# The head of a two-layer attention and mixer kernel, put into another order: tokens first, then each weight ahead of its own matmuls, the other loads tied to steps

## The chip, the cores and the metric

The kernel runs on one core of a Trainium2 chip. The metric is device microseconds for one execution of the whole program, the median of several executions. Five engines work side by side, each on its own list of instructions in its own order: TensorE (PE in the profile, its weight loads PEld), VectorE (DVE), ScalarE (ACT), GpSimd (POOL) and SyncE (SP), which issues all DMA transfers of this kernel. An instruction that waits holds everything behind it on its engine.

## What is computed

Four sublayers follow one another on 2048 tokens of width 640: attention A, mixer B, A again with the same weights, B again. Each is added to its input, and each takes a normalised input.

```python
x = x + A(layernorm(x)); x = x + B(layernorm(x))
x = x + A(layernorm(x)); x = x + B(layernorm(x))

# A: 32 heads of 20, four segments of 512 tokens, one after another
for s in range(4):
    p = softmax(q_s k_s^T * scale + mask)            # within the segment
    a_mem = phi(q_s) M / (phi(q_s) z + 1e-6)         # memory of the segments before
    o_s = g * a_mem + (1 - g) * (p v_s)
    M, z = M + phi(k_s)^T v_s, z + sum(phi(k_s))
y = o @ wo
# B: z1, z2 = halves of gelu(x @ w_in);  y = (z1 * (w_sp @ layernorm(z2) + b_sp)) @ w_out
```

## The kernel before, in words

**Precision.** A matmul of float32 precision is made of three float16 matmuls. Every operand is split into a high half and a low half: the high half is the float16 of the scaled value, the low half what is left. A weight's scale is a power of two taken from its largest absolute value. For one weight this takes (lines 48 to 73): a reduction of each 128-row piece, a reduction over the pieces (`wam`), `pow2_scales` with a transpose and a small matmul on TensorE (`wtp`, `wbc`, lines 52 and 58) and some eight tiny VectorE operations that end in `iv` (line 65), and then per piece one ScalarE operation for the high half (line 72) and one VectorE operation for the low half (line 73).

**Head.** `prologue` (line 117) loads wv, wq and wk, in that order, each as five tiles of 320 KB (line 135), and scales and splits them in the order v, q, k (lines 136 to 145). It then derives some scalars from the scales of q and k (lines 150 to 165). In `Attention.run`, for the first layer (`self.stacked < 0`, line 1030), `prep` loads 128 tokens (line 607), takes statistics (line 202, then a power on POOL, line 205), normalises (line 615), splits (line 217 on ScalarE, 218 on POOL) and turns the halves by a transposing DMA (line 219, tile `xt`). `start` fills the constant rows of the five `qk` buffers (lines 585 and 586). Then `early` computes four value tiles (`value`, line 621) and units 0 and 1 (`unit`, line 678).

**Units and values.** A unit m of segment s is 128 feature columns of q and of k for 512 tokens: 15 matmuls for q, then 15 for k (line 689). Both accumulate in the PSUM pool `pd`, tag `dn`, two banks. `out` (line 694) evicts them: high half on ScalarE, low half on VectorE, and for k the feature map phi too (lines 705, 711, 713, 722, 723), which writes into the bank in place and so holds it until line 723 is done. The halves go to a buffer in DRAM (`stack`, lines 798 and 799). A value tile is 128 tokens by 640 columns in two halves of 15 matmuls (line 632), also in `dn`.

**The step loop.** The 64 pairs of heads are worked off in steps t, three steps for each pair, from t = -10 (`-LEAD`) on. `fetch` (line 803) brings the pair's q and k rows into one of five `qk` buffers. `scores` (line 829) makes, for pair n, score blocks in `es` (one pair of banks, `pe`) which ScalarE turns into exponentials `P` (line 864), and, two pairs ahead, blocks in `mp` (one pair of banks, `px`) whose row maxima VectorE takes (`mx`, line 871). `maxes` (line 885) sends the maxima into the `qk` buffer by two small DMAs (line 894). `cast` splits `P` into `PH` (ScalarE, line 881) and `PL` (POOL, line 882); `pvs` multiplies with the values (line 908).

Beside the steps run four streams, each with a due time in steps: `fills` (token preps and the reads of `o`), `background` (the scales and splits of the remaining weights), `dense` (the units, values and output projections of later segments, in an order written out by hand, with a pace in ns of matmul per step) and `reads` (the memory). `until` (line 1043) takes what is due.

`background` begins at step 6. In the first layer `other_scales` (line 168) loads 32 tiles of wo, w_in and w_out (`wmst`, line 179, two buffers) and reduces each on VectorE (`wap`, lines 181 and 185), at 1.2 steps from tile to tile in program order; at step 53 come the scales, from step 55 on the splits of `wo` and of the second half of `w_in`.

**What sets the order.** Only TensorE follows the program's order (`manual_schedule(engines=ENGINES)`, line 1085). For the other engines and for the DMA queue of SyncE a planner orders the instructions when the program is built: it takes, among those that it believes ready, the one that was traced first, and `high_priority` makes instructions count as traced earlier. So in the kernel before, the 32 `wmst` loads, which wait for nothing but their two buffers, were put far ahead of step 6: the trace has the first reduction at 23.9 us and the last at 112.7 us.

## Time and profile before

| what | value |
|---|---|
| timed executions | 2472.66, 2474.31, 2476.86 us; median 2474.31 |
| span of the profiled execution, from the first to the last instruction | 2466.8 us |
| median less the span (what lies around it) | 7.5 us |
| instructions in the profile | 50722 |
| first value matmul | 36.17 us |
| first unit of step -10 | 88.30 us |
| first score matmul of step 0 | 134.39 us |

The profile is of one execution, with its own times in us from the start of the span; the page has no other time of that execution than the span. A row of the timeline gives start, duration, engine, line and operation, the tile written and read, how many instructions were merged, and in brackets how long the engine stood idle before and what released it. Line L207 means line 207 of the kernel. SPq rows are the issues of DMAs, not the transfers.

### The profile page before, as it was taken

What the parts mean: (1) busy time and instruction counts of PE and PEld (TensorE: products, weight loads), DVE (VectorE), ACT (ScalarE), POOL (GpSimd) and SP (SyncE); (2) the same over time, 40 slices, a digit from 0 to 9 for tenths busy, and PEclk for the clock granted to TensorE, in tenths of its full rate; (3) what the DMA queues carried; (4) which work ended last, traced back from release to release, by engine and by line L of the source; (5) the groups of instructions that cost most, each with busy time, mean ns of one, the idle gap of its engine ahead of it and who ended that gap; (6) DMA issues with size and microseconds to landing.
All of it is one profiled execution on the core that took longest, in us unless ns stands there. A gap on an engine that the chain in (4) does not pass through costs nothing.

```text
span 2466.8 us, 50722 instructions
## 1 busy us (share of the span) xinstructions
PE 2224.2 (90%) x20682; PEld 1317.4 (53%) x20682; DVE 1431.5 (58%) x2766; ACT 1137.3 (46%) x1388; POOL 937.1 (38%) x728
## 2 busy tenths in 40 slices
PE   3688888999899989999997888889997997999998
PEld 2355455666545545555554545565664554555554
DVE  8667877677754545544326777777764453453441
ACT  3278767777632222212124977777772222121110
POOL 3168777888610100000012988788872110000000
PEclk9899899999999999999999999999998998999999
DMA  6724644334553487767444352443446345766762
GB/s 198 207 56 101 172 107 113 100 108 123 140 162 94 114 221 193 189 155 173 101 137 124 74 123 69 112 113 86 126 128 145 94 114 151 167 166 155 173 128 58
DMA packets 502505, 325.00 MB, mean 132 GB/s; under 512 B 408512, under 2 KB 443456, under 8 KB 497152
## 3 DMA queue, kind: packets, MB, share of 16 engines
q1 hardware_dynamic: 502272, 321.76, 50.8%
q8 instruction: 162, 2.65, 0.5%
q14 instruction: 71, 0.58, 0.1%
HBM read 148.25 MB, written 85.34 MB: 95 GB/s over the span
## 4 chain that ended last, share of the span: by engine, by line
PE 56%; DVE 10%; ACT 10%; DMA 9%; issue 5%; SPq 3%; POOL 3%; ACTq 0%; DVEq 0%; POOLq 0%
PE gp L380 16%; PE zp L295 13%; PE cyp L409 6%; ACT PH L881 3%; ACT P L864 3%; PE vps L632 3%; PE pv L908 3%; DVE mx L871 3%; DMA wr<-in_B_w_sp_dram 2%; PE kps L689 2%; PE mp L855 2%; PE qps L689 2%; PE yps L665 2%; PE es L855 2%; POOL PL L882 2%
## 5 line engine op out<-in xcount | busy, mean ns | idle before, releaser
L882 POOL TENSOR_TENSOR PL<-P,PH 128x1280 f16<-128x1280 f32 x248 | 649.6, 2619 | 177.0 <-ACT PH L881 156.4
L380 PE MATMUL gp<-zh,wt 128*128 128x432 f16 x2048 | 466.6, 348 | 23.8 <-DMA wt<-wn 23.8
L871 DVE TENSOR_REDUCE mx<-mp 128x2 f32<-128x1024 f32 (+3 forms) x512 | 409.4, 816 | 130.2 <-PE mp L827 127.4
L380 PEld LDWEIGHTS <-wt 128*128 128x128 f16 x3072 | 301.8, 98 | 286.4 <-DMA wt<-wn 25.5
L864 ACT ACTIVATE P<-es,sc 128x1024 f32<-128x1024 f32 (+1 forms) x384 | 371.3, 967 | 161.6 <-PE es L827 160.0
L881 ACT CAST PH<-P 128x1280 f16<-128x1280 f32 x256 | 320.5, 1253 | 19.2 <-PE pv L908 12.8
L295 PEld LDWEIGHTS <-th 128*128 128x128 f16 x1920 | 188.6, 98 | 178.6 <-issue 10.4
L380 PE MATMUL gp<-zl,wt 128*128 128x432 f16 x1024 | 272.8, 348 | 0.0
L395 POOL MEMSET un<- 128x64 f16 x32 | 4.8, 151 | 672.5 <-DMA ut<-un 610.2
L205 POOL TENSOR_TENSOR lnrs<-lnve,mhalf 128x1 f32<-128x1 f32 x96 | 58.5, 617 | 467.7 <-DVE lnve L204 442.9
L855 PEld LDWEIGHTS <-qk 60*128 60x128 f16 (+1 forms) x2048 | 91.4, 93 | 261.3 <-issue 155.6
L383 ACT ACTIVATE u<-gp,bsp,un 128x864 f32<-128x864 f32 x32 | 34.2, 1070 | 363.3 <-PE gp L380 363.3
L357 DVE TENSOR_REDUCE am<-wr 128x1 f32<-128x2048 f32 x32 | 73.2, 2286 | 218.6 <-DMA wr<-in_B_w_sp_dram 218.6
L855 PE MATMUL mp<-qk 60*128 60x512 f16 (+3 forms) x1024 | 138.3, 307 | 55.9 <-DVE mx L871 55.0
L632 PE MATMUL vps<-wvh,xt 128*128 128x320 f16 x640 | 157.5, 310 | 27.2 <-DMA xt<-xnhl 14.5
L409 PE MATMUL cyp<-wuh,ut 128*128 128x320 f16 (+1 forms) x896 | 166.8, 303 | 11.9 <-DMA ut<-un 11.9
L855 PE MATMUL es<-qk 64*128 64x512 f16 (+3 forms) x1024 | 134.3, 298 | 47.3 <-ACT P L864 34.7
L409 PEld LDWEIGHTS <-ut 128*128 128x128 f16 (+1 forms) x1344 | 132.8, 99 | 69.9 <-DMA ut<-un 13.5
L827 PEld LDWEIGHTS <-big 64*128 64x128 f16 x3072 | 141.0, 95 | 50.5 <-issue 3.2
L908 PE MATMUL pv<-vs,PL 128*128 128x41 f16 x2560 | 163.0, 181 | 4.9 <-DVE PL L882 2.6
L908 PE MATMUL pv<-vs,PH 128*128 128x41 f16 x2560 | 166.3, 182 | 1.2 <-DVE ab L924 1.2
L295 PE MATMUL zp<-wi1h,th 128*128 128x432 f16 x640 | 150.2, 349 | 8.8 <-DMA th<-xnhl 8.8
(182 smaller groups left out, 4063.7 us busy)
## 6 DMA issues: line engine op xcount, KB each, us to landing
wr<-in_B_w_sp_dram SPq DMA_DIRECT2D x32, 1024.0 KB
qk<-st SPq DMA_DIRECT2D x256, 120.0 KB
x<-x SPq DMA_DIRECT2D x56, 320.0 KB
z<-z SPq DMA_DIRECT2D x32, 432.0 KB
cz<-z SPq DMA_DIRECT2D x32, 432.0 KB
xt<-in_A_x_dram SPq DMA_DIRECT2D x32, 320.0 KB
st<-qhl SPq DMA_DIRECT2D x40, 256.0 KB
st<-khl SPq DMA_DIRECT2D x40, 256.0 KB
```

The source lines that it names most:

```text
L295: nc.tensor.matmul(zp[:, n, :FHH], a[:, k, :], b[:, k, c:c + FHH], start=(k == 0 and j == 0), stop=(k == KD - 1 and j == 2))
L380: nc.tensor.matmul(gp[:, n, :FHH], wt[:, k // 8, a, k % 8, :], b[:, k, n * FHH:(n + 1) * FHH], start=(k == 0 and j == 0), stop=(k == NT - ...
L409: nc.tensor.matmul(yp[:, n, :320], a[:kn[k], k, :], b[:kn[k], k, n * 320:(n + 1) * 320], start=(k == 0 and j == 0), stop=(k == KO - 1 and ...
L632: nc.tensor.matmul(ps, a[:, k, c], b[:, k, n * 320:(n + 1) * 320], start=(i == 0), stop=(i == 14))
L689: nc.tensor.matmul(ps, a[:, k, c], b[:, k, :], start=(i == 0), stop=(i == 14))
L827: nc.tensor.matmul(out, g.big[r, 64 - 64 * s:192 - 64 * s], mk, start=False, stop=s == 1, skip_group_check=True)
L855: nc.tensor.matmul(out[:, h, o:o + w], a[r, ac], b[r, bc], start=o == 0, stop=False, skip_group_check=True)
L864: nc.scalar.activation(P[:, :, 512 * c:512 * c + ew], es[:, :, :ew], AF.Exp, scale=g.esc)
L871: nc.vector.tensor_reduce(self.mx[m][:, :, i], mp[:, :, o:o + w], AX.X, ALU.max)
L881: nc.scalar.copy(PH, P[:, h])
L882: (nc.gpsimd if h == 0 or n < self.N - self.TAIL else nc.vector).tensor_tensor(PL, P[:, h], PH, ALU.subtract)
L908: nc.tensor.matmul(pv[:, i, h, :], x[:, c:c + 128], v[:, j, h0 + h, :], start=(j == 0 and x is PH), stop=(j == i and x is PL), skip_group_ ...
```

## The change

The head is a new method of `Attention`, `head`, which takes the place of `prologue`'s loads and splits and of the first layer's `prep`, `start` and `early`.

- *Order of loads on SyncE*: four token tiles into one buffer `xs` (a buffer of `P`), the five tiles of wq, the first two turns, the five tiles of wk, the other two turns, then wv. wk is issued after the second turn and wv after the fourth (`issue_after` adds an order without a wait on data, on the engine that issues).
- *Tokens* are normalised and split into `xhl`, one buffer for all four tiles (a second buffer of `P`).
- *q* is scaled and split after the second token tile in program order. Then TensorE has q's matmuls of units 0 and 1, both m, in the bank pair of `es`; then k's scale, split and matmuls in the bank pair of `mp`; then v's scale and split, `start`, and the four value tiles in `dn`.
- *The split of k and v*: pieces 1 and 3 of five are done as a multiplication in place and a copy on ScalarE and a subtraction on POOL, instead of one ScalarE and one VectorE operation.
- *The rest*: the scalars (`attn_scalars`) come after k's split; the load of `bsp` and the clearing of `wap` move to step 6; the interval of `other_scales` becomes 1.45 steps; what the streams `fills` and `background` issue on SyncE is put behind the last fetch or row of maxima traced so far, in both layers; the pools `topi` and `topo` are opened after the head instead of before.

```diff
-def prologue(g, ctx, wv, wq, wk, wo, w_in, w_out):
+def attn_weights(g, ctx, wv, wq, wk, wo, w_in, w_out):
...
+    def head(self):
+
+        g, nc, tc = self.g, self.nc, self.tc
+        abs_max = lambda out, a: nc.vector.tensor_reduce(out, a, AX.X, ALU.max, apply_absolute_value=True)
+        with ExitStack() as ctx:
+            p = ctx.enter_context(tc.tile_pool(name="wpro", bufs=1, side="right", reuse_waits="tile"))
+            ctx.enter_context(tc.high_priority(offset=HP))
+            xs = self.p3.tile([128, 4, D], F32, tag="P", name="xs")
+            hl = self.p3.tile([128, 4, 2, D], F16, tag="P", name="xhl")
+            for t in range(4):
+                nc.sync.dma_start(xs[:, t], self.x[t])
+            st = {nm: p.tile([128, KD, D], F32, name="wst" + nm) for nm in "qkv"}
+
+            def load(nm):
+                for k in range(KD):
+                    self.sp = nc.sync.dma_start(st[nm][:, k, :], g.raw[nm][k * 128:(k + 1) * 128, :]).ins
+
+            def scale(nm):
+                i = WNAMES.index(nm)
+                am = g.wam[:, i:i + 1]
+                a = p.tile([128, KD], F32, tag="wamk", name="wamk")
+                for k in range(KD):
+                    abs_max(a[:, k:k + 1], st[nm][:, k])
+                nc.vector.tensor_reduce(am, a, AX.X, ALU.max)
+                pow2_scales(g, self.pl1, self.pm, "ms", g.wam, i, 1)
+
+            def split(nm):
+                h, l = g.w[nm]
+                for k in range(KD):
+                    if nm == "q" or k % 2 == 0:
+                        split_scaled(g, h[:, k], l[:, k], st[nm][:, k], WNAMES.index(nm))
+                    else:
+                        w = st[nm][:, k]
+                        nc.scalar.mul(w, w, g.iv[:, WNAMES.index(nm):][:, :1])
+                        nc.scalar.copy(h[:, k], w)
+                        nc.gpsimd.tensor_tensor(l[:, k], w, h[:, k], ALU.subtract)
+
+            last = None
+            for t in range(4):
+                mv, rs = layernorm_stats(g, xs[:, t], D, 2, XS)
+                nc.vector.tensor_scalar(xs[:, t], xs[:, t], mv[:, 0:1], rs, ALU.subtract, ALU.mult)
+                nc.scalar.copy(hl[:, t, 0], xs[:, t])
+                nc.gpsimd.tensor_tensor(hl[:, t, 1], xs[:, t], hl[:, t, 0], ALU.subtract)
+                o = self.xt[0][:, :, :, t * 128:(t + 1) * 128]
+                if t % 2 == 0:
+                    with tc.issue_after(last) if last is not None else ExitStack():
+                        load("qk"[t // 2])
+                last = nc.sync.dma_start(o.rearrange("p i k c -> p (i k) c"), hl[:, t].rearrange("p i c -> p (i c)"), transpose=True).ins
+                if t == 1:
+                    scale("q")
+                    split("q")
+            with tc.issue_after(last):
+                load("v")
+            qp = self.pe.tile([128, 2, 512], F32, tag="es", name="qp")
+            kp = self.px.tile([128, 2, 512], F32, tag="mp", name="kp")
+            for nm, ps in (("q", qp), ("k", kp)):
+                if nm == "k":
+                    scale("k")
+                    split("k")
+                    attn_scalars(g)
+                for m in range(2):
+                    for _ in self.unit(0, m, {nm: ps[:, m]}):
+                        pass
+            scale("v")
+            split("v")
+            self.start()
+            for t in range(4):
+                for _ in self.value(t):
+                    pass
...
-        for nm in ("q", "k"):
+        for nm in ("q", "k") if own is None else own:
             wh, wl = g.w[nm]
-            ps = self.pd.tile([128, L], F32, tag="dn", name=f"{nm}ps")
+            ps = self.pd.tile([128, L], F32, tag="dn", name=f"{nm}ps") if own is None else own[nm]
...
             if not g.wo.made:
+                nc.sync.dma_start(g.bsp, self.b_sp.rearrange("(t p) -> p t", p=128))
+                nc.vector.memset(g.wap, 0.0)
                 for i, _ in enumerate(other_scales(g, self.bg, self.pl1, self.pm, "ms")):
-                    yield 6 + 1.2 * i if _ else 53
+                    yield 6 + 1.45 * i if _ else 53
...
         if self.stacked < 0:
-            for t in range(0, 4, 2):
-                for f in zip(self.prep(t), self.prep(t + 1)):
-                    f[0]()
-                    f[1]()
-                if t == 0:
-                    self.start()
-            for i in range(4, 8):
-                self.early(i)
+            self.head()
         else:
             self.start()
+        g = self.g
+        g.top = [self.top.enter_context(g.tc.tile_pool(name=n, bufs=1, side="right", reuse_waits="tile")) for n in ("topi", "topo")][::-1]
...
-                e[0] = next(e[2], None)
+                with self.tc.issue_after(self.sp) if e[1] < 2 and self.sp is not None else ExitStack():
+                    e[0] = next(e[2], None)
```

In `fetch` and `maxes`, `self.sp` is set to the DMA that was just issued.

58 lines of the change are left out of this document (21 added, 37 removed).

## The prediction

> **What bounds the kernel now.** I read the page first, then the busy times by stage, then the timeline of the first 140 us engine by engine, then the waits, and last the same stages of the second attention layer, which the program enters around 1290 us without the loads that this change moves.
>
> The page's first line says that TensorE is busy 90% of the span. So time can be had only where it stands still, and the busy times by stage say where (columns: stretch, its length, then busy us of PE, PEld, DVE, ACT, POOL with counts, granted clock, DMA share, GB/s).
>
> ```profile
> PE 2224.2 (90%) x20682; PEld 1317.4 (53%) x20682; DVE 1431.5 (58%) x2766; ACT 1137.3 (46%) x1388; POOL 937.1 (38%) x728
> ...
> 0.00:36.20 36.20, 4.46 (x16) 3.18 (x17) 33.08 (x88) 9.76 (x14) 8.42 (x28) 1.00 0.69 217
> 36.20:88.30 52.10, 36.24 (x181) 19.38 (x181) 35.77 (x88) 17.91 (x30) 18.17 (x19) 0.90 0.78 198
> 88.30:134.40 46.10, 34.14 (x206) 16.56 (x206) 25.24 (x42) 8.66 (x16) 0.55 (x1) 0.85 0.59 163
> 134.40:240.00 105.60, 92.24 (x1409) 56.39 (x1405) 78.47 (x149) 92.09 (x116) 86.87 (x48) 0.98 0.34 82
> 1292.30:1335.80 43.50, 31.68 (x202) 15.60 (x200) 26.46 (x51) 11.19 (x20) 7.79 (x8) 0.88 0.62 157
> ```
>
> Until 36.2 us TensorE does almost nothing while VectorE is full (33.1 of 36.2). From 36.2 to 88.3 it does the four value tiles and units 0 and 1; from 88.3 to 134.4 it leads in (steps -10 to -1); at 134.4 the first scores of step 0 start. Everything after is a chain on that start. The boundaries, in the timeline (start, us, engine, line, operation, and the wait in brackets):
>
> ```profile
> 36.17 0.45 PE L632 MATMUL vps<-wvh,xt 128*128 128x320 f16 x1 [9.23 <-DMA xt<-xnhl]
> 88.30 0.59 PE L689 MATMUL qps<-xt,wqh 128*128 128x512 f16 x2
> 88.95 0.59 PE L689 MATMUL qps<-xt,wqh 128*128 128x512 f16 x2
> 134.39 0.38 PE L855 MATMUL es<-qk 64*128 64x512 f16 x2
> ```
>
> The first value matmul waits for the first turned tokens, not for a weight. 88.30 to 88.95 is the price of three unit matmuls at full clock, 0.65 us; a unit's fifteen for q or k take 3.2 us.
>
> **The change part by part.** *Head.* The same work in another order: tokens, then q, then k, then v. TensorE's order is the program's, so the rise has three links in a row: q's matmuls, k's scale, split and matmuls, v's scale, split and matmuls. The durations:
>
> ```profile
> 9.82 0.16 DVE L139 TENSOR_REDUCE wam<-wamk 128x1 f32<-128x5 f32 x1
> 14.98 0.14 DVE L65 TENSOR_SCALAR iv<-iv 128x1 f32<-128x1 f32 x1
> 5.30 0.82 DVE L138 TENSOR_REDUCE wamk<-wstv 128x1 f32<-128x640 f32 x1
> 9.00:12.00 3.00, 0.58 (x2) 0.29 (x3) 3.00 (x9) 0.00 (x0) 0.00 (x0) 1.00 1.03 404
> 28.98 0.88 DVE L73 SCALAR_TENSOR_TENSOR wql<-wstq,iv,wqh 128x640 f16<-128x640 f32 x1
> 36.86 3.70 ACT L72 ACTIVATE wkh<-wstk,iv 128x640 f16<-128x640 f32 x5
> 37.03 1.40 POOL L218 TENSOR_TENSOR xnhl<-xt,xnhl 128x640 f16<-128x640 f32 x1 [4.40 <-ACT xnhl L217]
> 57.77 1.33 SPq L219 DMA_TRANSPOSE xt<-xnhl  x1
> 61.18 0.31 PE L632 MATMUL vps<-wvh,xt 128*128 128x320 f16 x1 [1.42 <-DMA xt<-xnhl]
> 61.32 0.30 PE L632 MATMUL vps<-wvl,xt 128*128 128x320 f16 x1
> 61.73 0.30 PE L632 MATMUL vps<-wvl,xt 128*128 128x320 f16 x1
> 109.67 1.01 PE L689 MATMUL kps<-xt,wkh 128*128 128x512 f16 x2 [8.34 <-DVE phl L723]
> 110.91 1.06 PE L689 MATMUL kps<-xt,wkh 128*128 128x512 f16 x2
> ```
>
> q: the first transfer can be reduced at 5.3 us, and at 404 GB/s a 320 KB tile lands each 0.82 us; q's five stand behind four of tokens, so the ninth is in at 11.9 and reduced at 12.7. The scale chain took 5.3 us for v (9.82 to 15.1): 18.0. The split is paced by VectorE, five of 0.88 us after ScalarE's first 0.74: 23.1. The tokens: POOL's 1.40 us subtraction and a 3.4 us turn (57.77 to 61.18) end each tile, and tiles 2 and 3 are written behind q's scale and split, so I put the last turned tile at 25 us; q's matmuls need all four. Thirty matmuls take 6.5 us, and after a long idle time three cost 1.24 us instead of 0.65 for some 4 us (109.67 to 110.91), 1.8 more: **33**.
>
> k: its loads wait on SyncE behind the second turn, at some 13 us, and land by 20 (five of 0.82, and the turns between); v's, behind the fourth, by 30. Both are early. But its two small matmuls of the scale follow q's on TensorE: the chain begins at 33; fewer other VectorE operations are left, 4 us: 37. The split puts seven ScalarE operations of 0.74 us in a row (two of five pieces take a multiplication and a copy), then 0.88 on VectorE: the first k unit ends at 43.3, the second, partly at the low clock, at **48**.
>
> v: chain again, now beside the k units' eviction on VectorE, 5.3: 53.3. The first half value is paced by the split, 6.3: 59.6. Seven halves of fifteen (three cost 0.41 us, 61.32 to 61.73) take 14.4, the low clock about 2: **76**. Against 88.3 that is 12 us earlier. Bounds: 66, if the chains overlap better (3 us each, as no filler stands between their operations), and 84, if each is as long as k's was:
>
> ```profile
> 24.66 0.14 DVE L139 TENSOR_REDUCE wam<-wamk 128x1 f32<-128x5 f32 x1
> 36.43 0.14 DVE L65 TENSOR_SCALAR iv<-iv 128x1 f32<-128x1 f32 x1
> ```
>
> That was 11.9 us, with splits and reductions between every two of its operations. I take 76, since v's own chain (5.3) is the nearest row.
>
> The early units in the scores' banks cost nothing: the scores ask for them only in the lead-in, and they spare the value tiles a wait for a bank. The new copies on ScalarE are in the sum. The fill of the `qk` buffers moves behind v's split:
>
> ```profile
> 38.41 4.59 POOL L586 TENSOR_SCALAR qk<-wkh,keep 128x512 f16<-128x512 f16 x5
> 42.42 3.17 ACT L585 ACTIVATE qk<-wkh,qrow 128x512 f16<-128x512 f16 x5 [1.53 <-DVE qrow L158]
> ```
>
> It lies beside 14 us of value matmuls; without them the first fetch would come 4.6 us later. `bsp`'s load and the clearing of `wap` only change place. The first prep of the next tokens goes behind the first fetch; v4 is 5 steps later, so a 3.3 us load is covered; without that cover TensorE would wait those 3.3 us.
>
> *Lead-in, 46.1 us now.* Here the weights' loads are in the way today:
>
> ```profile
> 102.06 0.82 DVE L181 TENSOR_REDUCE wap<-wmst 128x1 f32<-128x640 f32 x1 [5.54 <-DMA wmst<-in_B_w_out_dram]
> PE kps L689 <- DVE phl L723: 17.7, 4, 8.3
> L181 DVE TENSOR_REDUCE wap<-wmst x31: 547/603/821, 23.9 to 111.4; 128x1 f32<-128x432 f32 x20, 128x1 f32<-128x640 f32 x11
> ```
>
> VectorE stands 5.5 us for a load, and behind it waits the k eviction that frees a bank. Yet the same stage in layer 2 has no such loads and takes 43 us (1292.3 to 1335.1, the table's last row): another wait ends last there. So only some **4 us** go.
>
> *First segment, 105.6 us now.* The 32 reductions come here, at 1.45 steps apart from step 6. There are 31 in the row above and one more of 96 partitions: twenty at its median of 0.6 us, twelve at its 0.8, 21.6 us in all, 1.4 us per pair of heads. VectorE goes from 78.5 to 100.1 of 105.6 us. It is the engine that frees the one bank pair of `mp`, and TensorE stands in order behind that:
>
> ```profile
> PE mp L855 <- DVE mx L871: 6.3, 13, 1.0
> 135.25 1.12 ACT L864 ACTIVATE P<-es,sc 128x1024 f32<-128x1024 f32 x1
> 239.10 1.11 ACT L864 ACTIVATE P<-es,sc 128x1024 f32<-128x1024 f32 x1 [2.78 <-PE es L827]
> ```
>
> Fifteen pairs take 103.9 us, 6.9 each. At 95% use, a reduction often stands just ahead of a maximum. Each reduction also comes some 3 us after its own load (1.45 steps of 2.3), and a load of this size needs 3.4 us from issue to reader:
>
> ```profile
> 270.19 0.59 SPq L607 DMA_DIRECT2D xt<-in_A_x_dram  x1
> 273.60 0.89 DVE L202 BATCH_NORM_STATS2 lnst<-xt 128x6 f32<-128x320 f32 x2 [0.76 <-DMA xt<-in_A_x_dram]
> ```
>
> so some of them will make VectorE stand. Bounds: 2 us lost (all in its 27 us of idle time) and 34 (21.6 added whole, and 0.4 of standing each). I take **9**, two fifths of the work.
>
> Ahead of the reductions in SyncE's queue now stand the fetch and the row of maxima; a blocked fetch holds the load, and the load holds a reduction. Behind step 53 the loads of `wo` and `wi1` come at their steps instead of two being early, and layer 2's prep loads may no longer run ahead: I take 0 for both, bounds 3 either way, for a token load is read 3.4 us after its issue and has 11 steps.
>
> The sum: 12 + 4 - 9 = 7 us less. The profiled span is 2466.8, the median 2474.3; the 7.5 us around the span stay. Span 2460, time **2467**.
>
> *A rule weighed.* VectorE and POOL do collide in this trace:
>
> ```profile
> 328.76 2.62 POOL L882 TENSOR_TENSOR PL<-P,PH 128x1280 f16<-128x1280 f32 x1
> 328.92 2.92 DVE L73 SCALAR_TENSOR_TENSOR wi1l<-wst,iv,wi1h 128x432 f16<-128x432 f32 x1
> 398.56 2.62 POOL L882 TENSOR_TENSOR PL<-P,PH 128x1280 f16<-128x1280 f32 x1 [0.81 <-POOL lnrs L205]
> 399.89 0.89 DVE L202 BATCH_NORM_STATS2 lnst<-xt 128x6 f32<-128x320 f32 x2 [1.57 <-DMA xt<-in_A_x_dram]
> ```
>
> An operation with two SBUF operands that starts inside a PL subtraction takes 2.92 us, not 0.6; two statistics with one operand, inside another PL, take their usual 0.89. No row shows a reduction from SBUF under PL, and POOL is in PL four fifths of the first segment. The Trainium skill, "SBUF — State Buffer", section "Who interferes with whom", states that on trn2 a `tensor_reduce` never contends with GpSimd. By that rule the sum stays as it is, and only the loads' half of rival 3 is left.
>
> **The rivals.** (1) *Reductions hidden.* VectorE's 27 us of idle time takes them: loss 2, so 12 + 4 - 2 = 14 less, **2460**; for it, ScalarE (92.1 of 105.6) and TensorE are closer to the bound; against it, TensorE already waits for the maxima. (2) *No difference.* The loss is 16, as most of the moved work lands on the path: **2474**. (3) *Slower, by stalls on VectorE* in the first segment: each of 32 reductions holds VectorE about 1 us more, for its load (3.4 us against 3) or for POOL's port (half of 2.6 us). Then the loss is 21.6 + 32 less some 20 that fall into idle time: 34, so 18 more, **2492**. It decides from a stall of about 0.5 us each. Against it: the statistics row. (4) *The head isn't shorter*: chains of 11.9 us, start at 84: 4 + 4 - 9, **2475**.
>
> **How the numbers follow.** Forecast 0.40 (its own band 2460 to 2472), rival 1 0.20, rival 2 0.14, rival 3 0.16, rival 4 0.10. This kernel's measurement tells about 0.2%, 5 us, from nothing. Of the forecast's 0.40, 0.34 is beyond that and 0.06 within; with rival 1 faster is 0.54. Within: those 0.06, rival 2, and half of rival 4, 0.25. Slower: rival 3 and the other half of rival 4, 0.21. The range goes from 2448 (start at 66, loss 9, lead-in 4, and some) to 2488, which leaves out the far half of rival 3 and the best of rival 1.
>
> **What would show it.** In the changed profile: the first q matmul at about 25 us, the first k at 38, the first value at 54; step -10's first unit (the fifth group of q matmuls, `dn` bank) at 76; first `es` at 118; 32 `wap` reductions spread from step 6 to 51; pairs of the first segment 7.5 us apart instead of 6.9. A first `es` later than 128 would make the head wrong; `wap` reductions of 2 us the port; `wap` waiting for `wmst` by more than 15 us the loads.

## The result and the profile after

The changed kernel takes **2510.2 us** (median of 4 runs, 2502.63 to 2510.85) beside 2473.48 us of the kernel before (4 runs): ratio 1.0148, 95% interval 1.0127 to 1.0170. It is slower by 36.7 us. The forecast was 2467, the range ended at 2488, and the slowest rival stood at 2492. The profiled execution of after took 2509.89 us with a span of 2508.1, so 1.8 us lie around it; before's span was 2466.8, and the spans differ by 41.3. In every execution on record 1.7 to 2.1 us lie around the span: the 7.5 us that I put there for before are mostly that its profiled execution was some 5 us shorter than its median.

The busy times of after by stage (stretch, its length, busy us of PE, PEld, DVE, ACT, POOL with counts, granted clock, DMA share, GB/s), cut where after's own stages end:

```profile
0.00:26.20 26.20, 2.51 (x9) 1.99 (x9) 21.70 (x64) 8.25 (x12) 13.54 (x33) 1.00 0.83 229
26.20:94.20 68.00, 40.73 (x186) 20.44 (x187) 33.63 (x74) 23.02 (x37) 17.38 (x15) 0.75 0.37 101
94.20:131.20 37.00, 33.17 (x207) 16.34 (x206) 16.17 (x26) 7.37 (x14) 0.00 (x0) 0.91 0.24 69
131.20:254.00 122.80, 92.14 (x1373) 56.03 (x1367) 90.93 (x176) 91.97 (x115) 85.45 (x49) 0.96 0.47 121
```

TensorE starts 10 us earlier than before (26.2 against 36.2) and then needs 68.0 us for the matmuls that took 52.1, at a granted clock of 0.75 instead of 0.90: the head is full of holes. Its boundaries in the timeline of TensorE:

```profile
70.46 0.43 PE L689 MATMUL vps<-wvh,xt 128*128 128x320 f16 x1 [3.89 <-ACT wvh L72]
...
94.21 0.59 PE L746 MATMUL qps<-xt,wqh 128*128 128x512 f16 x2
...
131.18 0.38 PE L912 MATMUL es<-qk 64*128 64x512 f16 x2
```

First value matmul 70.5, step -10 at 94.2 (before: 88.3), first scores at 131.2 (before: 134.4). So the start of step 0 moved by 3.2 us, not by 16.

For the rest I follow one row per pair of heads: the start of the pair's last exponential, the only one of 512 columns. A segment has 16 pairs, so pair 15 is the last of the first segment; between pair 41 and the end nothing large happens. Pairs 0, 15 and 41 of layer 1, before and then after, in the timeline of ScalarE:

```profile
139.79 0.68 ACT L864 ACTIVATE P<-es,sc 128x512 f32<-128x512 f32 x1
...
244.04 0.69 ACT L864 ACTIVATE P<-es,sc 128x512 f32<-128x512 f32 x1 [0.47 <-PE es L827]
...
491.51 0.69 ACT L864 ACTIVATE P<-es,sc 128x512 f32<-128x512 f32 x1 [0.70 <-PE es L827]
```

```profile
136.58 0.68 ACT L921 ACTIVATE P<-es,sc 128x512 f32<-128x512 f32 x1
...
262.08 0.69 ACT L921 ACTIVATE P<-es,sc 128x512 f32<-128x512 f32 x1
...
527.12 0.69 ACT L921 ACTIVATE P<-es,sc 128x512 f32<-128x512 f32 x1 [1.29 <-PE es L884]
```

Pairs 0 to 15 take 125.5 us instead of 104.25 (+21.2), pairs 15 to 41 take 265.0 instead of 247.5 (+17.6). After that the two run nearly even: the last pair of layer 2 is 39.6 us late. Three places, then: head and lead-in -3.2, first segment +21.2, the next segments +17.6.

Read in the same rows of each run's own timeline, all runs of this study, as us later (+) or earlier than before at pairs 0, 15, 41 and the last (128th):

| run | what is changed | ratio to before, 95% | 0 | 15 | 41 | last |
|---|---|---|---|---|---|---|
| after | | 1.0148 [1.0127, 1.0170] | -3.2 | +18.0 | +35.6 | +39.6 |
| e2_lag | reductions traced two loads later | 1.0170 [1.0147, 1.0193] | -2.1 | +20.3 | +35.3 | +43.7 |
| e3_no_reduce | no reductions | 1.0039 [1.0024, 1.0055] | -1.9 | -3.8 | +9.0 | +12.6 |
| e12_lag4 | reductions four loads later and behind mx | 1.0088 [1.0073, 1.0103] | -5.0 | -3.7 | +15.4 | +20.4 |
| e9_act_queue | loads on ScalarE's queue | 1.0096 [1.0076, 1.0115] | +10.1 | +7.5 | +21.0 | +26.4 |
| e7_no_hold | nothing held | 1.0033 [1.0020, 1.0046] | +13.9 | +13.7 | +12.4 | +16.5 |
| e6_fills_free | background held alone | 1.0086 [1.0067, 1.0104] | -5.0 | +13.4 | +17.9 | +23.8 |
| e1_bg_free | fills held alone | one execution, 2483.55 us | +10.9 | +8.0 | +15.2 | +15.4 |
| e4_banks | a tile for each head unit | 1.0088 [1.0071, 1.0104] | -12.3 | +5.6 | +23.6 | +26.9 |
| e16_fill | fill behind v's split | 1.0115 [1.0096, 1.0134] | -9.4 | +9.7 | +26.1 | +26.2 |
| e8_before_hold | before, with the hold | 1.0117 [1.0100, 1.0134] | -13.5 | +4.7 | +22.3 | +26.2 |
| b1_before_no_reduce | before, no reductions | 0.9977 [0.9962, 0.9991] | -3.8 | -3.1 | -4.1 | -2.3 |
| e5_lead | e4, loads in the lead-in, nothing else held | 1.0024 [1.0013, 1.0035] | +6.8 | +8.8 | +7.2 | +10.2 |
| e13_mix | e4, e12, less held | 1.0002 [0.9991, 1.0013] | -7.5 | -5.9 | +3.9 | +15.4 |
| e17_all | e4, e16, e12, loads held in segment 1 alone | 1.0053 [1.0036, 1.0070] | -12.4 | +0.2 | +0.9 | +6.9 |
| e18_before_lag | before's head with e17's loads | 0.9986 [0.9974, 0.9999] | -17.6 | -7.3 | -3.3 | +5.5 |

Each row is read from one profiled execution; the farthest from the medians of the timed ones are before's and e17's, some 5 us under, and e13's, 6 above. Runs whose head is the same (after, e2, e3, e12) differ by up to 3.1 us at the first pair, so I read nothing into less than that.

### The profile page after: what moved, and what is told of

Read it like the earlier page. It is cut to its first block, busy times and chain, and to the rows that moved or that the text cites. A ratio compares the mean times of both kernels' runs of the same rounds, so it can differ in the third digit from the quotient of the medians.

```text
span 2508.1 us, 50684 instructions
## 1 busy us (share of the span) xinstructions
PE 2240.5 (89%) x20682; PEld 1327.2 (53%) x20682; DVE 1437.9 (57%) x2762; ACT 1143.2 (46%) x1392; POOL 947.0 (38%) x732
## 5 line engine op out<-in xcount | busy, mean ns | idle before, releaser
L366 PE MATMUL gp<-zh,wt 128*128 128x432 f16 x2048 | 466.6, 348 | 23.8 <-DMA wt<-wn 23.8
L395 PEld LDWEIGHTS <-ut 128*128 128x128 f16 (+1 forms) x1344 | 133.2, 99 | 74.7 <-DMA ut<-un 17.6
L353 ACT ACTIVATE wn<-wr,ivw 128x1024 f16<-128x1024 f32 x64 | 72.0, 1146 | 185.2 <-DVE ivw L348 107.4
```

What stands on the lines that cost most here:

```text
L366: nc.tensor.matmul(gp[:, n, :FHH], wt[:, k // 8, a, k % 8, :], b[:, k, n * FHH:(n + 1) * FHH], start=(k == 0 and j == 0), stop=(k == NT - ...
L395: nc.tensor.matmul(yp[:, n, :320], a[:kn[k], k, :], b[:kn[k], k, n * 320:(n + 1) * 320], start=(k == 0 and j == 0), stop=(k == KO - 1 and ...
```

## The experiments

### The first segment: a loop through two queues

My theory at first: each reduction `wap` of the moved stream stands on VectorE for its own load, and `mx` queues behind it. The waits of after between 131 and 255 us point that way (engine and line, what was waited for: us, times, longest), and the tile's own view gives the reductions' durations:

```profile
PE mp L912 <- DVE mx L928: 25.7, 23, 3.0
...
DVE wap L167 <- DMA wmst<-in_B_w_in_dram: 17.0, 10, 2.2
```

```profile
L167 DVE TENSOR_REDUCE wap<-wmst x31: 553/603/821, 155.5 to 273.8; 128x1 f32<-128x432 f32 x20, 128x1 f32<-128x640 f32 x11
```

VectorE waits 17.0 us in ten stands of up to 2.2 for the pieces of w_in alone (21.3 for all pieces up to pair 15), TensorE stands 25.7 us for `mx` (10.2 in the same stretch of before), and the reductions themselves are as short as before (603 ns).

**e2_lag**: a third buffer, and each reduction traced two loads after its own.

```diff
-                if last is not None:
-                    nc.vector.tensor_reduce(*last, AX.X, ALU.max, apply_absolute_value=True)
-                last = g.wap[:n, i, j:j + 1], t
+                lag.append((g.wap[:n, i, j:j + 1], t))
+                if len(lag) > 2:
+                    nc.vector.tensor_reduce(*lag.pop(0), AX.X, ALU.max, apply_absolute_value=True)
...
```

> After, with each of the 32 reductions wap traced two loads later than its own load (a third staging buffer), so that VectorE's queue reaches a reduction when its data have long landed; the same 32 reductions of 0.60 us stay where they hold up the steps, and the loads stay held to SyncE's steps. Theory A (the pairs 0 to 15 are 21 us longer, 125.5 against 104.3, because VectorE stands some 2.2 us at most reductions for a load issued in the same step, and mx of the next pair queues behind it): the waits of wap on wmst fall from 19.8 us to under 3, the pairs 0 to 15 take 106 to 112 us, the time falls by 14 to 20 to 2490 to 2496. Rival B (the work of the reductions itself, 32 x 0.60 us on a VectorE that sets the pace): the pairs stay at 122 to 126 us, the time at 2507 to 2511.

Nothing changed: 2513.8 us, pairs 0 to 15 take 126.6, and the stands for loads, which were to fall under 3 us, are 19.3 (131 to 256 us). A pair of loads and the reduction of the first of them, in e2's timeline:

```profile
170.30 0.86 SPq L165 DMA_DIRECT2D wmst<-in_B_w_in_dram  x2
...
172.80 0.60 DVE L168 TENSOR_REDUCE wap<-wmst 128x1 f32<-128x432 f32 x1 [1.69 <-DMA wmst<-in_B_w_in_dram]
```

Counted from the first load, the two at 170.30 are the seventh and the eighth, and the reduction at 172.80 is the seventh: the lag is in the program, and on the chip it is gone, since SyncE's queue runs that much behind VectorE's. So e2 did not test its theory; it asked what holds SyncE. One pair of after, in the timeline of all engines:

```profile
168.25 0.51 SPq L951 DMA_DIRECT2D qk<-mr  x1
...
168.86 0.82 SPq L165 DMA_DIRECT2D wmst<-in_B_w_in_dram  x2
...
171.37 0.60 DVE L167 TENSOR_REDUCE wap<-wmst 128x1 f32<-128x432 f32 x1 [2.15 <-DMA wmst<-in_B_w_in_dram]
171.89 1.22 DVE L928 TENSOR_REDUCE mx<-mp 128x2 f32<-128x1024 f32 x1
...
175.64 0.27 DVE L949 SCALAR_TENSOR_TENSOR mr<-mtp,mr 8x128 f16<-8x128 f32 x1
...
175.94 0.52 SPq L951 DMA_DIRECT2D qk<-mr  x1
...
176.50 0.86 SPq L165 DMA_DIRECT2D wmst<-in_B_w_in_dram  x2
...
184.25 0.83 SPq L165 DMA_DIRECT2D wmst<-in_B_w_in_dram  x2
```

This is a **closed loop**. The load stands on SyncE behind the write `qk<-mr` to which the change ties it (168.25, then 168.86). It is read 2.5 us later (171.37). Behind that reduction VectorE does the maxima and, last, the low half of `mr` (175.64). That releases the next write (175.94), and only then the next load goes out (176.50). Once round is 7.64 us, then 7.75 (184.25). Over all 15 intervals of the segment, those with a unit's evictions among them, after needs 8.37 us and before 6.95.

**e3_no_reduce** keeps the 32 loads and leaves the reductions out (the scales of wo, w_in and w_out then come from a constant, so that part of the computation is missing). **e12_lag4** keeps both but puts the reduction four loads behind its load and, by an order on VectorE's own queue, behind the newest `mx`.

```diff
-                if last is not None:
-                    nc.vector.tensor_reduce(*last, AX.X, ALU.max, apply_absolute_value=True)
...
-                nc.vector.memset(g.wap, 0.0)
+                nc.vector.memset(g.wap, 1.0)
```

```diff
+                lag.append((g.wap[:n, i, j:j + 1], t))
+                if len(lag) > 4:
+                    with g.tc.issue_after(g.mxi):
+                        nc.vector.tensor_reduce(*lag.pop(0), AX.X, ALU.max, apply_absolute_value=True)
...
```

> After, with the 32 reductions wap left out and their loads kept in place (the scales of wo, w_in and w_out then come from a constant, so that part of the computation is missing). Theory A (standing for own loads plus the work, both on VectorE): pairs 0 to 15 come down from 125.5 to 103 to 106 us, the time to 2488 to 2491; with e2 it tells the work (the difference of the two) from the standing. Rival C (the 32 loads' transfers, 0.8 us each of SyncE's queue and 221 KB each, hold up the folds and score operands that go by the same queue): pairs stay at 120 or more, time over 2503. The further 17 us of pairs 16 to 41 stay in both.

> After, with each reduction wap traced four loads behind its own load (five staging buffers) and put in VectorE's queue behind the newest reduction mx, so that it can't be drawn forward to its own load as it was in e2; loads, bytes, their hold to SyncE's steps and the 32 reductions of 0.60 us stay. Theory G (per pair a loop: SyncE's write qk<-mr, then the load, its landing 2.5 us later, the reduction wap that VectorE stands for, mx, mr, the next write): the waits of wap on wmst fall from 22.1 us to under 3, pairs 0 to 15 come from 125.5 to 104 to 110 us, the time falls by 14 to 20, to 2489 to 2496. Rival B (the reductions' own 21.6 us on VectorE): pairs stay above 118, time above 2502. What pairs 16 to 41 lose stays in both.

e3: pairs 0 to 15 take 102.35 us, the time is 2481.8; both are a little under what was expected, and pairs 15 to 41 lose 12.8 us where 17 were to stay. So the loads themselves (rival C) cost nothing in the first segment. e12, the timeline at pairs 0 and 15, and its waits between 131 and 255 us:

```profile
134.75 0.68 ACT L923 ACTIVATE P<-es,sc 128x512 f32<-128x512 f32 x1
...
240.39 0.66 ACT L923 ACTIVATE P<-es,sc 128x512 f32<-128x512 f32 x1
```

```profile
PE mp L914 <- DVE mx L930: 9.8, 17, 1.9
...
DVE wap L173 <- DMA wmst<-in_B_w_out_dram: 3.1, 1, 3.1
```

105.6 us with all loads in place and 26 of the 32 reductions inside these pairs (28 in after): 1.4 more than before, 3.3 more than e3. The wait for loads is down to one of 3.1, behind pair 15. It is shown, then, that nearly all of the first segment's 21.2 us comes from where the reductions stood, just behind their own loads and ahead of `mx`, and not from their work. Rival B is out. The stands that went, 21.3 us, are as long as what was won, 19.9; but e12 changes the lag and the place behind `mx` together, and no run tells the two apart. That the stands close into a loop is read off the rows of after; no run opens the loop at SyncE's end.

**e9_act_queue** was to open the loop another way, with the loads on ScalarE's queue (`nc.scalar.dma_start`).

> After, with the 32 loads wmst issued from ScalarE's queue instead of SyncE's, everything else kept (the same hold to the steps, the same 32 reductions, the same bytes). Theory G (a loop once per pair: on SyncE the load stands behind the writes qk<-mr of the step that it is held to, those wait for mr, which comes from mx, and mx stands on VectorE behind the reduction that waits for the load; the loop of 7.6 us sets the pace of pairs 0 to 15): with the load on another queue the loop is open, the waits of wap on wmst fall from 19.8 to under 6 us, pairs 0 to 15 take 106 to 112 us instead of 125.5, and the time comes to 2491 to 2499, with 32 issues of 0.4 us on ScalarE (13 us) as the price that it may show in part. Rival H (the landing of 2.2 to 2.5 us behind any issue, whatever queue): waits and pairs stay, 2505 to 2513.

It missed its purpose. The tile's view:

```profile
L167 DVE TENSOR_REDUCE wap<-wmst x31: 580/603/820, 11.4 to 81.6; 128x1 f32<-128x432 f32 x20, 128x1 f32<-128x640 f32 x11
```

The order behind a SyncE instruction doesn't bind another queue, so all loads ran in the head, and the first pair is 10.1 us late; the first segment, free of them, takes 101.7 us. The time, 2496.9, fell where it was expected, for another reason.

### The hold alone, and what the later segments lose

**e8_before_hold** is before with nothing of the new head, only the hold and the pace of 1.45.

```diff
...
-                e[0] = next(e[2], None)
+                with self.tc.issue_after(self.sp) if e[1] < 2 and self.sp is not None else ExitStack():
+                    e[0] = next(e[2], None)
```

> Before, its head untouched, with the fills and the background stream held behind SyncE's latest step as in after, and the loads wmst at after's pace: the one part of the change that the theory blames, alone. Theory G (the hold makes the loss, whatever the head): pairs 0 to 15 take 118 to 126 us instead of 104.3, pairs 16 to 41 lose 10 to 18, and the time is 2495 to 2508 with a gain of 4 to 8 us before the first pair, whose head then lacks the loads and reductions. Rival (the hold costs only with the new head's queues): 2466 to 2480.

2496.7 us, as theory G has it. In TensorE's timeline its step -10 and its first scores:

```profile
75.15 0.59 PE L690 MATMUL qps<-xt,wqh 128*128 128x512 f16 x2
...
120.92 0.38 PE L856 MATMUL es<-qk 64*128 64x512 f16 x2
```

The first segment loses 18.1 us (21.2 in after) and pairs 15 to 41 lose 17.6, as in after. So the hold makes these losses on the old head too. But the gain ahead of the first pair was put too low: its first scores come at 120.9, **13.5 us ahead of before's and 10.3 ahead of after's**. The old head, freed of the loads and reductions, beats the new one. All of it lies ahead of step -10, which starts at 75.15 instead of 88.30; its lead-in takes 45.8 us, before's 46.1.

**e7_no_hold**, **e6_fills_free** and **e1_bg_free** are after with the hold taken from both streams, from the fills, and from the background (`e[1] < 0`, `e[1] == 1` and `e[1] == 0` in the line above).

> After, with neither the fills nor the background stream held behind SyncE's steps: the new head with the loads placed freely, as before has them. Theory A (hold of the background = +21 in pairs 0 to 15; what is lost in pairs 16 to 41, +17, and in layer 2, +2 to 3, also comes from holding the two streams): the time comes to 2466 to 2476, pairs 0 to 15 take 103 to 108 us. Rival E (the later 17 us come from elsewhere, for instance the changed order of layer 1's evictions or the odd halves of the clock): 2485 to 2492 with the first segment back at 104 to 108. Rival F (free loads crowd into the head): the first es is later than 131.2 by some 10 us and that is lost again.

> After, with only the background stream held to SyncE's steps and the fills (the loads of the next tokens and their preparations) free as in before. Theory I (the 13 to 17 us lost in pairs 16 to 41 of layer 1 and the 2 to 3 of layer 2 come from the held fills): the first segment stays at 125 us, the later loss falls from 17 to under 4 us, and the time comes to 2493 to 2500. Rival J (they come from the held loads of wo and w_in, which belong to the background): the time stays at 2507 to 2512.

> After, with the background stream free and only the fills held: one look at pairs 16 to 41 of layer 1 and at layer 2, for the split of the late loss between the two held streams (with fills free and the background held it was 4.5 and 5.7 us, with both held 17.6 and 3, with neither 0 and 1). If the fills make it: 9 to 14 us in pairs 16 to 41 and at most 2 in layer 2; if it needs both held: under 4. The head is 10 to 17 us longer, since the loads wmst then stand in it, and the first segment free of loss; time 2480 to 2495.

e7 lies between theory A and rival E in time, 2479.6, because rival F came true: first pair 13.9 us late, for the loads stand in the head again. From there to pair 41 it loses nothing. Pairs 15 to 41, against before's 247.5 us:

- neither held: -1.3 (e7) and -1.5 (e5);
- background alone: +4.5 (e6); fills alone: +7.3 (e1, one execution);
- both: +17.6 (after), +17.6 (e8), +18.0 (e4), +19.1 (e12), +15.0 (e2), +16.4 (e16), +13.5 (e9) and +12.8 (e3);
- nothing held but the loads of `wmst`, before the scales: +9.8 (e13), +0.7 (e17) and +4.0 (e18), nearly all of it by pair 32.

So the later loss is the hold too, and the two streams together cost more than the sum of each. It comes in two places. After is 18.0 us late at pair 15, 29.3 at pair 22, only 21.0 at pair 32, and 35.6 at pair 41. The waits of pairs 15 to 22, before (244 to 320 us) and after (262 to 349):

```profile
ACT wi1h L72 <- DMA wst<-in_B_w_in_dram: 4.4, 2, 2.9
ACT woh L72 <- DMA wst<-in_A_wo_dram: 3.4, 2, 2.5
...
DVE lnst L202 <- DMA xt<-in_A_x_dram: 0.8, 1, 0.8
```

```profile
ACT ohl L992 <- DMA xt<-xnhl: 9.2, 2, 7.3
...
ACT woh L72 <- DMA wst<-in_A_wo_dram: 7.8, 3, 4.4
...
DVE lnst L188 <- DMA xt<-in_A_x_dram: 5.2, 3, 3.5
```

ScalarE's stands for pieces of weights are the same in sum, 7.8 us: before has them for wo and w_in, after for wo alone. New are 9.2 us in which ScalarE stands with the output half `ohl` for the turn of a held token tile, since `ohl` and `xnhl` share one buffer (tag `xh`), and VectorE's stands for tokens are 5.2 us instead of 0.8. But most of what these pairs lose is made good by pair 32. The larger step is pairs 32 to 41: +14.6 in after, +14.2 in e8, +7.0 in e6, +5.7 in e1, +0.6 in e7. There the stands for loads are hardly longer than before's, so they don't explain it; in after the last of the ten splits of w_in's second half starts as late as 521.5 us (before: 328.2), but e1 loses its 5.7 us with that split long done (408.1; its pair 32 starts at 423.3). How the hold becomes time in these pairs stays open. Theory I nearly holds in e6 (4.5 left of 17.6; the time, 2491.3, is a little under its 2493 to 2500) and is too simple by e1, where the fills alone make 7.3. Pair 41 to the last loses 4.0 in after, 4.2 in e7 with nothing held, 0.2 in e1: no part of the change is shown to make it.

### The head

**e4_banks** gives each head unit its own PSUM tile.

```diff
-            qp = self.pe.tile([128, 2, 512], F32, tag="es", name="qp")
-            kp = self.px.tile([128, 2, 512], F32, tag="mp", name="kp")
+            qp = [self.pd.tile([128, L], F32, tag="dn", name=f"qp{m}") for m in range(2)]
+            kp = [self.pe.tile([128, 2, 512], F32, tag="es", name="kp0")[:, 0], self.px.tile([128, 2, 512], F32, tag="mp", name="kp1")[:, 0]]
```

> After, with the four head units each in a PSUM tile of its own (q's in the two buffers of dn, k's in a bank of es and a bank of mp) instead of two halves of one tile. Theory A (the second unit's first matmul waits 2.62 and 4.95 us for the eviction of the other half, though it writes another bank): both waits go, q's matmuls end near 34.5 instead of 37.1, the second k unit near 54 instead of 61.2, the values near 87 instead of 94.2, time down 6 to 8 to 2502 to 2504. Rival D (the next thing is late anyway: k's split behind the fill of qk, v's chain behind the layernorm stats of the next tokens): the values end at 92 or later and the time falls by less than 3.

In after, TensorE's timeline in the head, and GpSimd's and VectorE's:

```profile
33.85 0.59 PE L746 MATMUL qp<-xt,wqh 128*128 128x512 f16 x2 [2.62 <-DVE qhl L763]
...
37.09 0.27 PE L52 MATMUL wtp<-ident,wam 128*1 128x128 f32 x1
...
47.23 0.61 PE L746 MATMUL kp<-xt,wkl 128*128 128x512 f16 x1 [2.25 <-POOL wkl L624]
...
55.85 1.01 PE L746 MATMUL kp<-xt,wkh 128*128 128x512 f16 x2 [4.95 <-DVE phl L780]
...
61.23 0.27 PE L52 MATMUL wtp<-ident,wam 128*1 128x128 f32 x1
...
65.99 0.58 PE L58 MATMUL wbc<-wdg,ones 1*128 1x1 f32 x2 [4.49 <-DVE wdg L56]
```

```profile
40.50 5.31 POOL L573 TENSOR_SCALAR qk<-wkh,keep 128x512 f16<-128x512 f16 x5 [21.08 <-ACT wkh L72]
45.78 1.39 POOL L624 TENSOR_TENSOR wkl<-wstk,wkh 128x640 f16<-128x640 f32 x1
```

```profile
39.40 0.14 DVE L65 TENSOR_SCALAR iv<-iv 128x1 f32<-128x1 f32 x1
...
59.20 0.89 DVE L188 BATCH_NORM_STATS2 lnst<-xt 128x6 f32<-128x320 f32 x2 [3.40 <-DMA xt<-in_A_x_dram]
...
64.14 1.68 DVE L672 TENSOR_SCALAR xt<-xt,lnmv,lnrs 128x640 f32<-128x640 f32 x1 [0.55 <-POOL lnrs L191]
...
68.48 0.15 DVE L65 TENSOR_SCALAR iv<-iv 128x1 f32<-128x1 f32 x1
```

The second unit's first matmul waits 2.62 us for q and 4.95 for k on the eviction of the *other* half of its tile, though it writes a bank of its own. In e4 both waits are gone, and step -10 and the first scores come 9.0 and 9.1 us earlier than in after:

```profile
85.21 0.59 PE L746 MATMUL qps<-xt,wqh 128*128 128x512 f16 x2
...
122.09 0.38 PE L912 MATMUL es<-qk 64*128 64x512 f16 x2
```

The time falls by 0.0060 of before's 2473, 15 us; expected were 6 to 8. In the traces 9.1 of it is ahead of the first pair and some 3 fall in the first segment. The Trainium skill, "Perfetto Trace Analysis", section "Matmuls", asks that independent groups rotate through PSUM banks so that the eviction of one overlaps the next one's matmuls. After keeps to that by banks and gains nothing; e4, with a tile for each group, gains the overlap. Here the tile decides, not the bank.

**e16_fill** puts the fill of `qk` behind the last piece of v's split on ScalarE's and GpSimd's queues.

```diff
+            with self.tc.issue_after(self.spl[0]) if self.spl else ExitStack():
+                nc.scalar.activation(t[:, 0], any_, AF.Identity, scale=0.0, bias=g.qrow)
+            with self.tc.issue_after(self.spl[1]) if self.spl else ExitStack():
+                nc.gpsimd.tensor_scalar(t[:, 1], any_, 0.0, g.keep[:, 2:3], ALU.mult, ALU.add)
...
```

> After, with the fill of qk (five writes of 0.64 us on ScalarE and of 1.06 us on GpSimd) put behind v's split on both queues, where in after it stands ahead of k's split. Theory M (the fill costs the first k unit the 2.25 us and more that PE waits for wkl, and the preparations of the next tokens that stood ahead of wvl cost v's split the same way): k's first unit ends near 46 instead of 50.9, the values end near 88 instead of 94.2, the time falls by 4 to 7, to 2503 to 2506. Rival N (the fill was hidden, other waits end at the same time): 2508 to 2511 and the values at 92 or later.

Step -10 in e16's timeline, and the first scores:

```profile
88.01 0.59 PE L748 MATMUL qps<-xt,wqh 128*128 128x512 f16 x2 [0.62 <-DVE vs L697]
...
125.00 0.38 PE L914 MATMUL es<-qk 64*128 64x512 f16 x2
```

6.2 us earlier than after, the time down by 0.0033 of 2473, 8 us, a little more than expected (the two intervals of the ratio overlap; the 6.2 us of the trace are the firmer figure). In after the fill (5.31 us on GpSimd at 40.50) is ahead of k's split, because the planner takes what it believes ready; the `wkl` piece that TensorE waits for starts at 45.78. Theory M holds for after. The two repairs don't add: e17 has both, and its step -10 starts at 86.62, e4's at 85.21.

**The lead-in** takes 37.0 us in after, 46.1 in before and 45.8 in e8. The waits in it, of before (88.3 to 134.4 us), e8 (75.1 to 120.9) and after (94.2 to 131.2):

```profile
PE kps L689 <- DVE phl L723: 10.1, 2, 8.3
```

```profile
PE kps L690 <- DVE phl L724: 10.0, 2, 5.1
...
DVE lnst L202 <- DMA xt<-in_A_x_dram: 8.7, 2, 5.5
```

```profile
PE kps L746 <- DVE phl L780: 2.0, 1, 2.0
```

TensorE stands for the k eviction that frees a bank: 10 us in before and e8, 2.0 in after, and that is 8.1 of the 9.1 us. In before VectorE stands 7.2 us here for loads of `wmst`, in e8 8.7 us for the tokens that it holds, in after for no load. The old head has a short lead-in too when VectorE stands for no load there: e18, which holds `wmst` alone, takes 37.8 us. This is read from the traces; no run changes it alone.

**b1_before_no_reduce** asks what before pays for its reductions in the head. As in e3 the scales come from a constant.

> Before, with its 32 reductions wap left out and the loads kept (the scales of wo, w_in and w_out come from a constant, so that part is missing). Theory K (before hides the reductions in the head, behind weight loads and VectorE's idle time there): 2468 to 2474, no difference. Rival L (they cost before about as much as they cost the new kernel wherever they stand, 17 to 21 us in e7's head, in e5's lead-in and in the first segment): 2450 to 2460.

5.2 us (2467.2 beside 2472.4), 3.8 of it ahead of the first pair: neither theory, nearer to K. Since e8's first pair is 13.5 us ahead with loads and reductions gone, some 10 are left for the loads, if the two add (an estimate; e8 holds other loads too, and by e18, 17.6 us ahead with these loads alone held, it is 14).

### Put together

**e5_lead** (e4, the background held only behind the head's last k write), **e13_mix** (e4 and e12, fills free), **e17_all** (e13 with e16, layer 2 not held, pace 1.2), and **e18_before_lag** (before's head with e17's treatment of the loads). The hold of e17 and e18:

```diff
+                with self.tc.issue_after(self.sp) if e[1] == 1 and not self.scaled and not self.g.wo.made and self.sp is not None else ExitStack():
```

> After with three changes: a PSUM tile for each unit of the head (as in e4), fills not held, and the background stream held only behind the last write of the head's k operand (about 55 us), so that the 32 loads and reductions fall into the lead-in from 55 to 125 us, where VectorE is 16 to 20 per cent busy. If the three causes add (head 9 to 12 us shorter than before's first es, 18 to 21 us of the first segment gone, 13 to 17 us of pairs 16 to 41 gone), the time is 2456 to 2464, faster than both kernels. Rival: the reductions and loads lengthen the lead-in, which then has them beside the early units' evictions on VectorE: 2466 to 2476, no better than before.

> After with a PSUM tile for each head unit (e4), the reductions four loads behind their loads and behind mx (e12), the fills and the loads of wo and w_in for good not held (e6 and more). If the three causes add: the first es comes 12 us ahead of before's (e4), pairs 0 to 15 lose 0 to 4 us, pairs 16 to 41 and layer 2 lose nothing: 2459 to 2466, faster than both kernels. Rival: the 21.6 us of reductions still hold VectorE at the place where the pairs have 1.4 us of slack each, and the first segment gives back 8 to 14: 2466 to 2476.

> After with every repair that a run here supports: a PSUM tile for each head unit (e4), the qk fill behind v's split (e16), fills and the permanent loads of the weights not held (e5, e7), the loads wmst held to the first segment alone with each reduction four loads behind and behind mx (e12), at a pace of 1.2 steps instead of 1.45, and layer 2 not held at all (e13 held it and lost 6.7 us there). If the parts add: first es 10 to 15 us ahead of before's, first segment even, up to 6 lost in pairs 16 to 41, layer 2 even: 2456 to 2466, faster than both kernels. Rival (what e13 lost in pairs 16 to 20, 8 us, comes from the late scale of wo, w_in and w_out and stays, and the shorter head is taken by the lead-in's own chain): 2466 to 2474.

> Before with its own head, the loads wmst held to the first segment of layer 1 at a pace of 1.2 steps, each reduction four loads behind and behind mx, and nothing else held: the treatment of e17 on the old head. Theory O (the new head, once mended, gives nothing that the old one does not have when its loads are out of the way: e8's first es is 13.5 us ahead, e17's 12.4): the same as e17 within 4 us, first es 11 to 14 ahead of before's, up to 13 given back in pairs 12 to 22, 2464 to 2476. Rival P (the new head is the better one): 6 or more above e17's span of 2472.7. If less is given back than in e17 it is faster than before: 2458 to 2464.

None of the three with the new head is faster than before. e5 takes the rival's course: with the 32 loads in the lead-in its first pair comes 19 us after e4's (+6.8 against -12.3). I had taken VectorE to be busy there for 16 to 20% of the time; in after it is 31.5 of the 70 us from 55 to 125. e13 ends at before's time; it lost 11.5 us after pair 41, with the background of layer 2 held. e17 starts 12.4 us ahead and has it all given back by pair 15; its 2479.7 us lie above even its rival's 2474. e18 starts furthest ahead, 17.6 us, keeps 3.3 of it at pair 41, and is the only one with all the work that lies under both kernels: 2468.1 beside 2472.3, ratio 0.9986 [0.9974, 0.9999]. That is 0.14%, less than the 0.2% that I called a difference; and in its one profiled execution the last pair is 5.5 us late and the span 2467.3, so where the timed runs have their 4 us the traces don't show. Rival P is out: the new head, mended, isn't better than the old one with the same loads; e17's span is 5.4 us longer than e18's, and its ratio higher.

e17 and e18 also bound what e12 showed: with the same lag, at a pace of 1.2, they lose 12.6 and 10.3 us up to pair 15. Of that 7.4 and 5.8 fall in pairs 13 to 15. There the last four reductions, which the edit leaves without the order behind `mx` (line 173 in e17, 187 in e18), stand for their loads again, 4.1 and 2.7 us. The order covers 28 of the 32; whether covering the rest would win this back no run shows.

## Why the prediction was wrong

Its sum was 12 (head) + 4 (lead-in) - 9 (first segment) + 0 (later) = 7 us less. In the traces the same terms are -5.9, +9.1, -21.2 and -17.6, and 4.0 are lost behind pair 41 for which there was no term.

- **"I take 9, two fifths of the work"** (first segment). Failed; it lost 21.2. I saw both parts (the work, and a load read 3.4 us after its issue at intervals of 3) and gave rival 3 a price of 34 for the two. But I let most of the standing fall into VectorE's idle time, and left SyncE's queue as a remark. e12 shows what is left of the loss when no reduction stands for its load: 1.4 us against before, 3.3 against e3. So the cost was where they stood, just behind their loads and ahead of `mx`, and VectorE's idle time did not absorb it. My signpost for the loads (`wap` waiting for `wmst` over 15 us) was right: 17.0 for those of w_in alone.
- **"I take 0 for both, bounds 3 either way"** (behind step 53). Failed; pairs 15 to 41 lost 17.6. My reason was that a token load has 11 steps. No rival had this loss. With the hold taken away it is gone (e7, e5), and the old head has it too (e8). After's largest new stands there are for held tokens (9.2 us at `ohl`, 5.2 at the statistics), but how most of it arises, in pairs 32 to 41, is open.
- **The head: q's matmuls done at 33, k's second unit at 48, values at 76.** It came to 37.1, 61.2 and 94.2, and the first scores at 131.2, past the 128 that I had named as the sign of a wrong head. The start of q's matmuls (26.2, 25 forecast) and the end of k's scale chain (39.4, 37 forecast) were right within 2.5 us. **"The early units in the scores' banks cost nothing"** failed (e4: 9 us), and **"It lies beside 14 us of value matmuls"** failed (e16: 6 us), for I assumed the fill's place in the program to be its place in the queue. v's chain took 7.3 us instead of 5.3, from 61.23 to 68.48, behind the next tokens' statistics on VectorE.
- **"So only some 4 us go"** (lead-in). 9.1 went. My row for the k eviction (17.7 us, four waits) was of a longer stretch; the lead-in has 10.1 of it, and 8.1 of that went. I set the limit by layer 2, whose same stage has no loads of weights; but there VectorE stands 6.6 us for its tokens, so it was no picture of a lead-in without stands. Less the head's loss of 5.9 it leaves the 3.2 us by which the first scores come earlier.
- **The rule weighed** agreed with the trace: by the Trainium skill, "SBUF — State Buffer", section "Who interferes with whom", reductions do not contend with GpSimd on trn2; here they take 553 to 821 ns beside a GpSimd that is busy for 85.45 of 122.8 us. What was left of rival 3, the loads' half, is what happened in the first segment, together with rival 4 (the head isn't shorter).

Two figures of the prediction are off without changing this: the lower end of the range, 2448, lies 9 us under what its terms give (22 + 4 - 9 from 2474), and the 7.5 us around the span are 1.7 to 2.1.

The direction failed because the new head's order gave no gain of its own: freed of the loads, the old head has step -10 at 75.15 (e8), the new one at 94.21. And the price of where the loads went was taken as work on one engine, when in the first segment it was waiting.

## What to carry to other kernels

When an instruction is tied behind another in a queue, follow what that one waits for: if it ends at the engine that reads the tied load, the way round can become the pace, however little work is in it. Look in the trace whether a lag between load and reader is still there: two loads in the program's order alone were gone (e2), four with an order on the reader's own queue held (e12). And before a head is rearranged, take its foreign traffic away from the old one and look.

## What the runs showed that I had not expected

In after's head TensorE ran at about half speed behind its pause of 4.95 us: two matmuls took 1.01 us at 55.85, and the fifteen up to 61.2 took 5.4 us, where those from 33.85 to 37.1 took 3.2. The head has a granted clock of 0.75 where before's had 0.90, so a hole there costs more than its length. The length of the last pause alone doesn't tell it: after 2.62 us the pace was full (0.59 at 33.85), after 2.12 and 1.97 it was half (1.03 at 40.46 and 43.95).

The 32 loads, some 0.4 us of queue each, are harmless beside the pairs (e3: 102.35 us for pairs 0 to 15), and in the head they cost 10 to 14 us, as estimated above from e8, b1 and e18. And 26 reductions cost 1.4 to 3.3 us in the first segment, once nothing waits for a load.
